# An adaLN block with hedgehog linear attention and a ReLU feed-forward on one core: the part before the feed-forward rewritten per 128-row tile, phi folded into weights, feed-forward matmuls reordered and interleaved

## The chip, the cores and the metric

The kernel runs on one core of a Trainium2 chip. The metric is the device time of that core in microseconds (us), lower is better. A time is quoted as a median of several runs; the profile belongs to one run, and its span is some 2 us shorter than the time of that run.

The engines are called as the profile calls them: PE is the matmul engine, PEld its weight load, DVE the vector engine, ACT the scalar (activation) engine, POOL the general engine, and SP, for which the pages show no busy time, issues transfers. "Granted clock" is the PE clock that the throttle allowed, 1.00 being full speed.

## The reference

S = 2048 rows, D = 576 features, 32 heads of 18, feed-forward width 4608, all bfloat16. Cut to what matters:

```python
sa, ca, ga, sb, cb, gb = split(silu(c) @ w_mod, 6)     # one row each
h = layernorm(x) * (1 + ca) + sa
q, k, v = heads(h @ wqkv)
pq, pk = q @ w_phi, k @ w_phi                          # 18x18 per head
phi_q = concat(softmax(pq), softmax(-pq))              # 36 features per head
phi_k = concat(softmax(pk), softmax(-pk))
kv, z = phi_k^T v, sum over rows of phi_k
o = (phi_q kv) / (phi_q z + 1e-6)
x = x + ga * (o @ wo)
h = layernorm(x) * (1 + cb) + sb
x = x + gb * (relu(h @ w1) @ w2)
```

576 is four and a half times 128. Both kernels therefore cut a contraction over features into four full matmuls over 128 features (`128*128` in the traces) and one "half" over 64 (`64*128`). They pair two halves, one in rows 0 to 63 and one in rows 64 to 127. For this pairing the kernels keep the last 64 features of each tensor a second time, in partitions 64 to 127.

## The kernel before

It runs in stages over the whole sequence. It loads all of x in one transfer, transposes it, computes the layernorm statistics with matmuls against ones, computes v, then loops over five groups of heads (seven heads, 126 columns, in a full one), computing q and k, phi, softmax and the attention of that group. Then come wo, a second layernorm over the whole sequence, and the feed-forward.

```python
nc.sync.dma_start(x_sb[:, :, :], xf.rearrange("(t p) d -> p t d", p=P))      # all of x
...
def dup_last_chunk():                      # the last 64 features again, by a transfer
    if PAIR:
        nc.gpsimd.dma_start(hT_sb[64:64 + kdl, cl, :], hT_sb[0:kdl, cl, :])
...
for g, (h0, nh) in enumerate(GRP):         # five head groups
    ...                                    # project q and k, cast them to qk_sb
    for tq in range(QT):                   # phi for q, then exp of both signs
        nc.tensor.matmul(pqp[0:nf, 0:SQ], lhsT=wbd[0:nf, 0:nf], rhs=qk_sb[0:nf, 0, sl], ...)
        nc.scalar.activation(out=Eq[0:nf, 0, sl], in_=pqp[0:nf, 0:SQ], func=ACT.Exp, scale=1.0)
        nc.scalar.activation(out=Eq[0:nf, 1, sl], in_=pqp[0:nf, 0:SQ], func=ACT.Exp, scale=-1.0)
    ...                                    # the same for k, its softmax, kv
    for tb in range(0, nT, NBN):           # both signs of q share ONE accumulator
        for sgn in range(2):
            nc.tensor.matmul(pnv[:, j, 0:nf + nh], lhsT=Eq[0:nf, sgn, t * P:(t + 1) * P],
                             rhs=KVZD[0:nf, sgn, 0:nf + nh], start=(sgn == 0), stop=(sgn == 1))
        ...                                # divide by one denominator per head
...                                        # transposes, dup_last_chunk, wo, second layernorm
dup_last_chunk()
for b in range(nTB):                       # feed-forward, 4 blocks of 512 rows
    while j < nKDF:                        # pairs of the 36 chunks of 128 hidden units
        for (jx, (js, jn)), hps in zip(js_list, hps_list):
            for ci, (st, kd) in enumerate(KD[:-1]):          # 8 full matmuls
                nc.tensor.matmul(hps[0:jn, :], lhsT=w1_sb[:kd, ci, js:js + jn],
                                 rhs=hT_sb[:kd, ci, b * TB:(b + 1) * TB], start=(ci == 0), stop=False)
        for idx, ((jx, (js, jn)), hps) in enumerate(...):    # 2 halves, rows 0 and 64
            b0 = 0 if idx == 0 else 64
            nc.tensor.matmul(hps[0:jn, :], lhsT=w1_sb[b0:b0 + kdl, cl, js:js + jn],
                             rhs=hT_sb[b0:b0 + kdl, cl, b * TB:(b + 1) * TB], start=False, stop=True)
        ...                                # relu, one chunk on ACT, one on DVE
    ...                                    # second matmul: 8 x 36 matmuls of 288 columns, then out
```

One detail of it is an approximation: the two softmaxes of q have normalisers of their own in the reference, while here the two signs are added without them and divided by one common denominator.

The softmax here doesn't subtract the row's maximum and nothing guards it: scores larger than these inputs give would overflow.

Of the kernel before, what the change touches and what calls it, by code (L numbers as in the profile page):

```python
# [7 lines left out]

STAGE = 99  # L10

P = 128
BF16 = mybir.dt.bfloat16
FP32 = mybir.dt.float32
EPS = 1e-5
# [3 lines left out]


def _chunks(n, c):
    out = []
    s = 0
    while s < n:
        out.append((s, min(c, n - s)))
        s += c
    return out
# [3 lines left out]
def kernel(  # L31
# [14 lines left out]
    B, S, D = A_x.shape  # L46
    assert B == 1
    H, Dh, _ = A_w_phi.shape
    Dff = B_w1.shape[1]
    assert D == H * Dh and Dh == 18, (D, H, Dh)  # L50
    nT = S // P
    assert S % P == 0
    KD = _chunks(D, P)
    nKD = len(KD)
    cl = nKD - 1
    stl, kdl = KD[cl]
    PAIR = (nKD >= 2 and kdl <= 64)
    KDF = _chunks(Dff, P)
    nKDF = len(KDF)
    NHG = P // Dh  # L60
    GRP = []
    hh = 0
    while hh < H:
        nh = min(NHG, H - hh)
        GRP.append((hh, nh))
        hh += nh
    NG = len(GRP)
    SQ = min(512, S)
    assert S % SQ == 0
    QT = S // SQ  # L70
    if S % 512 == 0:
        TB = 512
    elif S % 256 == 0:
        TB = 256
    else:
        TB = P
    nTB = S // TB
    NB = 4 if nT % 4 == 0 else (2 if nT % 2 == 0 else 1)
    CD = _chunks(D, 512)

    xf = A_x.flatten_outer_dims()
    outf = out.flatten_outer_dims()

    persist = ctx.enter_context(tc.tile_pool(name="persist", bufs=1))
    ident = persist.tile([P, P], BF16, name="ident")
    make_identity(nc, ident[:])
    onesb = persist.tile([P, P], BF16, name="onesb")
    nc.vector.memset(onesb[:], 1.0)
    eps_t = persist.tile([P, 1], FP32, name="eps_t")
    nc.vector.memset(eps_t[:], EPS)  # L90

    x_sb = persist.tile([P, nT, D], BF16, name="x_sb")
    nc.sync.dma_start(x_sb[:, :, :], xf.rearrange("(t p) d -> p t d", p=P))
    hT_sb = persist.tile([P, nKD, S], BF16, name="hT_sb")
    modcols = persist.tile([P, 6 * nKD], FP32, name="modcols")
    modrows = persist.tile([P, 2, D], FP32, name="modrows")
    mload = ctx.enter_context(tc.tile_pool(name="mload", bufs=1))
    ccol = mload.tile([P, nKD, 1], BF16, name="ccol")
    nc.vector.memset(ccol[:], 0.0)
    for ci, (st, kd) in enumerate(KD):  # L100
        nc.scalar.dma_start(ccol[:kd, ci, :], c[0:1, st:st + kd].rearrange("o k -> k o"))
    wmod_sb = mload.tile([P, nKD, 6 * D], BF16, name="wmod_sb")
    for ci, (st, kd) in enumerate(KD):
        nc.scalar.dma_start(wmod_sb[:kd, ci, :], w_mod[st:st + kd, :])

    actx = ExitStack()
    attn = actx.enter_context(tc.tile_pool(name="attn", bufs=1))
    wqkv_sb = attn.tile([P, nKD, 3 * D], BF16, name="wqkv_sb")
    for ci, (st, kd) in enumerate(KD):
        nc.sync.dma_start(wqkv_sb[:kd, ci, :], A_wqkv[st:st + kd, :])  # L110
    if PAIR:
        nc.sync.dma_start(wqkv_sb[64:64 + kdl, cl, :], A_wqkv[stl:stl + kdl, :])

    full_kd = [ci for ci, (st, kd) in enumerate(KD) if kd == P]
    assert nKD <= 8

    def transpose_tm_to_fm(src_tm_tile, t, pspool, dst):
        psraw = pspool.tile([P, 512], FP32, name="ps512")
        psT = psraw.bitcast(BF16)[:, 0:nKD * P].rearrange("p (c f) -> p c f", c=nKD)
        for ci, (st, kd) in enumerate(KD):  # L120
            nc.tensor.transpose(psT[:kd, ci, :], src_tm_tile[:, st:st + kd], ident[:, :])  # L121
        if full_kd:
            c0, c1 = full_kd[0], full_kd[-1] + 1
            nc.vector.tensor_copy(out=dst[:, c0:c1, t * P:(t + 1) * P], in_=psT[:, c0:c1, :])  # L124
        for ci, (st, kd) in enumerate(KD):
            if kd != P:
                nc.vector.tensor_copy(out=dst[:kd, ci, t * P:(t + 1) * P], in_=psT[:kd, ci, :])

    def dup_last_chunk():
        if PAIR:  # L130
            nc.gpsimd.dma_start(hT_sb[64:64 + kdl, cl, :], hT_sb[0:kdl, cl, :])

    def ln_pass1(rows_pool, pspool):
        xsq = rows_pool.tile([P, nKD, S], BF16, name="xsq", bufs=1)
        for ci, (st, kd) in enumerate(KD):
            nc.vector.tensor_tensor(out=xsq[:kd, ci, :], in0=hT_sb[:kd, ci, :], in1=hT_sb[:kd, ci, :], op=ALU.mult)
        ms, vs_ = [], []
        for tq in range(QT):
            sl = slice(tq * SQ, (tq + 1) * SQ)
            ps_s = pspool.tile([P, 512], FP32, name="ps512")  # L140
            ps_q = pspool.tile([P, 512], FP32, name="ps512")
            for ci, (st, kd) in enumerate(KD):
                nc.tensor.matmul(ps_s[:, 0:SQ], onesb[:kd, :], hT_sb[:kd, ci, sl],  # L143
                                 start=(ci == 0), stop=(ci == nKD - 1))
            for ci, (st, kd) in enumerate(KD):
                nc.tensor.matmul(ps_q[:, 0:SQ], onesb[:kd, :], xsq[:kd, ci, sl],  # L146
                                 start=(ci == 0), stop=(ci == nKD - 1))
            m = rows_pool.tile([P, 512], FP32, name="lnm")
            nc.scalar.activation(out=m[:, 0:SQ], in_=ps_s[:, 0:SQ], func=ACT.Copy, scale=1.0 / D)  # L149
            msq = rows_pool.tile([P, 512], FP32, name="lnmsq")  # L150
            nc.vector.tensor_tensor(out=msq[:, 0:SQ], in0=m[:, 0:SQ], in1=m[:, 0:SQ], op=ALU.mult)
            var = rows_pool.tile([P, 512], FP32, name="lnvar")
            nc.vector.scalar_tensor_tensor(out=var[:, 0:SQ], in0=ps_q[:, 0:SQ], scalar=1.0 / D,
                                           in1=msq[:, 0:SQ], op0=ALU.mult, op1=ALU.subtract)
            ms.append(m); vs_.append(var)
        lnvs = []
        for tq in range(QT):
            lnv = rows_pool.tile([P, 512], FP32, name="lnlnv")
            nc.scalar.activation(out=lnv[:, 0:SQ], in_=vs_[tq][:, 0:SQ], func=ACT.Ln, bias=eps_t[:], scale=1.0)
            lnvs.append(lnv)  # L160
        rss, nbs = [], []
        for tq in range(QT):
            rs = rows_pool.tile([P, 512], BF16, name="lnrs")
            nc.scalar.activation(out=rs[:, 0:SQ], in_=lnvs[tq][:, 0:SQ], func=ACT.Exp, scale=-0.5)  # L164
            rss.append(rs)
        for tq in range(QT):
            nb = rows_pool.tile([P, 512], BF16, name="lnnb")
            nc.vector.scalar_tensor_tensor(out=nb[:, 0:SQ], in0=ms[tq][:, 0:SQ], scalar=-1.0,
                                           in1=rss[tq][:, 0:SQ], op0=ALU.mult, op1=ALU.mult)
            nbs.append(nb)  # L170
        return rss, nbs

    def ln_apply(rows_pool, rss, nbs, scale_col, shift_col):
        for tq in range(QT):
            sl = slice(tq * SQ, (tq + 1) * SQ)
            rs, nb = rss[tq], nbs[tq]
            for ci, (st, kd) in enumerate(KD):
                t1 = rows_pool.tile([P, 512], BF16, name="lnt1")
                nc.vector.tensor_tensor(out=t1[:kd, 0:SQ], in0=hT_sb[:kd, ci, sl], in1=rs[:kd, 0:SQ], op=ALU.mult)  # L179
                nc.vector.tensor_tensor(out=t1[:kd, 0:SQ], in0=t1[:kd, 0:SQ], in1=nb[:kd, 0:SQ], op=ALU.add)  # L180
                if (tq * nKD + ci) % 2 == 0:
                    nc.scalar.activation(out=hT_sb[:kd, ci, sl], in_=t1[:kd, 0:SQ], func=ACT.Identity,  # L182
                                         scale=scale_col(ci, kd), bias=shift_col(ci, kd))
                else:
                    nc.vector.tensor_scalar(out=hT_sb[:kd, ci, sl], in0=t1[:kd, 0:SQ],  # L185
                                            scalar1=scale_col(ci, kd), scalar2=shift_col(ci, kd),
                                            op0=ALU.mult, op1=ALU.add)


    lctx1 = ExitStack()  # L190
    rows1 = lctx1.enter_context(tc.tile_pool(name="ln1rows", bufs=4))
    lnps1 = lctx1.enter_context(tc.tile_pool(name="ln1ps", bufs=4, space=bass.MemoryType.PSUM))
    for t in range(nT):
        transpose_tm_to_fm(x_sb[:, t, :], t, lnps1, hT_sb)
    rss1, nbs1 = ln_pass1(rows1, lnps1)

    with ExitStack() as mctx:
        modp = mctx.enter_context(tc.tile_pool(name="modp", bufs=1))
# [417 lines left out]
```

## Time and profile before

602.95 us, median of 4 runs (600.87 to 604.89).

These are lines of the page of the kernel before: its span, the busy time of PE with its share of the span, and three rows that cut the span into 40 equal slices (busy tenths of PE and DVE, and the granted clock in tenths).

```profile
span 602.0 us, 7761 instructions
...
PE 513.3 (85%) x3276; PEld 283.8 (47%) x3302; DVE 259.1 (43%) x589; ACT 148.5 (25%) x274; POOL 29.1 (5%) x36
...
PE   0899099799879598984089999999999999999997
...
DVE  0576934556956674797523211332123321133221
...
PEclk9995579797988759996679999999999999999999
```

85% busy looks almost full. The slices show two halves: PE is solid in the right half at clock 9, while the left half has gaps, and its clock sits between 5 and 9. The page therefore needs a table by stage. The next fence is the windows view of the kernel before: each row is a stretch of time, its length, the busy us of each engine with the number of instructions, the granted clock, and the share and rate of the transfers.

```profile
core 0: us, PE busy (x) PEld busy (x) DVE busy (x) ACT busy (x) POOL busy (x), PEclk, DMA share, GB/s
0.00:16.78 16.78, 0.00 (x0) 0.00 (x1) 0.35 (x4) 0.00 (x0) 3.79 (x28) 1.00 0.87 304
16.78:56.67 39.89, 38.33 (x288) 21.39 (x291) 25.84 (x64) 16.15 (x24) 0.00 (x0) 0.85 0.37 107
56.67:98.90 42.23, 27.49 (x157) 11.84 (x160) 28.50 (x64) 12.51 (x38) 0.66 (x1) 0.69 0.03 7
98.90:212.46 113.56, 92.80 (x631) 53.24 (x630) 69.51 (x156) 56.31 (x115) 23.60 (x5) 0.85 0.00 1
212.46:250.28 37.82, 34.98 (x232) 17.80 (x234) 22.61 (x68) 0.00 (x0) 0.57 (x1) 0.82 0.04 8
250.28:301.64 51.36, 25.00 (x137) 10.55 (x138) 38.10 (x99) 21.70 (x28) 0.51 (x1) 0.79 0.47 151
301.64:602.00 300.36, 294.72 (x1839) 169.02 (x1853) 74.16 (x136) 41.80 (x70) 0.00 (x0) 0.99 0.07 21
```

| stage (us) | what it does | PE idle, us | clock |
|---|---|---|---|
| 0 to 16.78 | load of x | 16.8 | - |
| 16.78 to 98.90 | transposes, statistics, modulation, v | 16.3 | 0.85, 0.69 |
| 98.90 to 212.46 | five head groups | 20.8 | 0.85 |
| 212.46 to 301.64 | wo, second layernorm | 29.2 | 0.82, 0.79 |
| 301.64 to 602.00 | feed-forward | 5.6 | 0.99 |

(PE idle is the length less the busy time.) Of 88.7 us of PE idle, 83 lie in the first half. The waits of PE in the kernel before, with what ended each, the total, how often, and the longest:

```profile
PE ps L121 <- DMA x_sb<-in_A_x_dram: 16.8, 1, 16.8
PE hps L560 <- DMA hT_sb<-hT_sb: 16.0, 1, 16.0
PE ps L315 <- ACT v_all L354: 14.4, 1, 14.4
PE hps L553 <- ACT hT_sb L182: 9.6, 1, 9.6
```

These four single waits make up 56.8 us: for x, for the copy of the last 64 features (it was issued at 294.6 us, when the whole second layernorm was done, and landed 7.0 us later), and twice behind a layernorm. The 9.6 us end with its last step. The 14.4 us end with an eviction of v that stands behind the first layernorm in the order of DVE and ACT; PE went on at 75.85 us. The weight load of its next halves waited for the first copy of the last 64 features until 75.99 us, so two waits end here almost together.

The feed-forward is bound by PE, and what can still be gained there is read in the timeline of PE (start us, us, line, shapes, how many; ends are modelled, so starts are to be compared). L553 are the full matmuls, L560 the halves:

```profile
312.38 0.39 PE L560 MATMUL hps<-hT_sb,w_sb 64*128 64x512 bf16 x2
312.70 1.90 PE L553 MATMUL hps<-hT_sb,w_sb 128*128 128x512 bf16 x8
314.53 0.39 PE L560 MATMUL hps<-hT_sb,w_sb 64*128 64x512 bf16 x2
```

A pair takes 314.53 - 312.38 = 2.15 us. Eight full matmuls and one slot of halves at 215 ns each are 1.94 us. The remaining 0.21 us are put down to two changes between full and half (changes of mode, or mode switches, below), some 0.107 us each: from the start of the halves to the next full matmul it is 0.32 us, about that much more than a slot.

### The profile page before, as it was taken

The numbers are of one execution on the slowest core, as the hardware profiler recorded it, in microseconds if no ns is written. First come the engines' busy times: TensorE is split into PE (matmuls) and PEld (weight loads), VectorE is DVE, ScalarE is ACT, GpSimd is POOL, SyncE is SP. The second block draws the span as 40 slices with busy tenths as digits, with TensorE's granted clock in tenths as the row PEclk, the third lists the DMA queues.
The fourth block names the chain that finished last, engine by engine and source line by source line (L and its number), as shares of the span: only waits on it lengthen the run. The fifth ranks groups of instructions, "written<-read, shape, count | busy, mean of one in ns | idle before, by whom it ended". The sixth has DMA issues, their size and how long they took to land.

```text
span 602.0 us, 7761 instructions
## 1 busy us (share of the span) xinstructions
PE 513.3 (85%) x3276; PEld 283.8 (47%) x3302; DVE 259.1 (43%) x589; ACT 148.5 (25%) x274; POOL 29.1 (5%) x36
## 2 busy tenths in 40 slices
PE   0899099799879598984089999999999999999997
PEld 0544044354444454531023577335773357733675
DVE  0576934556956674797523211332123321133221
ACT  0064322644644400046312100221002210022100
POOL 2000000013023200000000000000000000000000
PEclk9995579797988759996679999999999999999999
DMA  8910000000000000380380000000000000000000
GB/s 293 294 34 1 17 2 1 0 1 1 1 1 1 1 2 19 131 262 1 108 264 0 1 21 11 10 1 1 21 11 10 2 0 21 21 1 0 1 21 21
DMA packets 13651, 24.17 MB, mean 40 GB/s; under 512 B 2224, under 2 KB 11568, under 8 KB 12976
## 3 DMA queue, kind: packets, MB, share of 16 engines
q1 hardware_dynamic: 6704, 12.85, 6.5%
q10 hardware_dynamic: 6672, 10.03, 5.3%
q0 software_dynamic: 240, 0.79, 0.6%
q8 instruction: 26, 0.43, 0.3%
q14 instruction: 9, 0.07, 0.0%
HBM read 20.52 MB, written 2.36 MB: 38 GB/s over the span
## 4 chain that ended last, share of the span: by engine, by line
PE 56%; DVE 5%; ACT 1%; DMA 1%; issue 1%; DVEq 0%; POOLq 0%
PE hpsb L577 24%; PE hps L553 21%; PE hps L560 4%; PE ps L474 3%; PE ps L121 2%; DMA hT_sb<-hT_sb 1%; DVE lnt L180 1%; DVE lnt L179 1%; DVE hT_sb L124 1%; PE ps L146 1%; PE ps L143 1%; DVE hT_sb L185 1%; PE ps L481 1%; ACT L164 0%; PE psb L444 0%
## 5 line engine op out<-in xcount | busy, mean ns | idle before, releaser
L553 PE MATMUL hps<-hT_sb,w_sb 128*128 128x512 bf16 x560 | 139.5, 388 | 11.8 <-ACT hT_sb L182 9.6
L577 PE MATMUL hpsb<-w_sb,H 128*128 128x288 bf16 x1152 | 141.8, 286 | 0.0
L577 PEld LDWEIGHTS <-H 128*128 128x128 bf16 x1152 | 112.4, 98 | 29.1 <-issue 0.9
L566 ACT ACTIVATE H<-hps 128x512 bf16<-128x512 f32 x72 | 42.9, 597 | 227.5 <-PE hps L560 226.3
L568 DVE TENSOR_SCALAR H<-hps 128x512 bf16<-128x512 f32 x72 | 49.7, 691 | 113.7 <-PE hps L560 113.7
L553 PEld LDWEIGHTS <-w_sb 128*128 128x128 bf16 x576 | 51.5, 99 | 81.1 <-issue 31.9
L581 DVE TENSOR_TENSOR outt<-hpsb,modrows 128x288 bf16<-128x288 f32 x32 | 14.6, 457 | 116.3 <-PE hpsb L577 116.3
L370 PE MATMUL ps<-hT_sb,wqkv_sb 128*126 128x512 bf16 (+1 forms) x160 | 48.4, 442 | 2.1 <-ACT Ek L406 2.1
L560 PE MATMUL hps<-hT_sb,w_sb 64*128 64x512 bf16 x144 | 29.9, 394 | 16.0 <-DMA hT_sb<-hT_sb 16.0
L121 PE MATMUL ps<-ident,x_sb 128*128 128x128 bf16 (+1 forms) x160 | 20.8, 268 | 17.7 <-DMA x_sb<-in_A_x_dram 16.8
L315 PE MATMUL ps<-wqkv_sb,hT_sb 128*128 128x64 bf16 (+1 forms) x125 | 22.4, 324 | 15.8 <-ACT v_all L354 14.4
L370 PEld LDWEIGHTS <-wqkv_sb 128*126 128x126 bf16 (+1 forms) x160 | 21.6, 148 | 19.2 <-issue 12.3
L383 ACT CAST qk_sb<-ps 126x512 bf16<-126x512 f32 (+1 forms) x33 | 18.8, 592 | 46.4 <-PE ps L378 45.3
L124 DVE COPY hT_sb<-ps 128x512 bf16<-128x512 bf16 x48 | 20.3, 423 | 22.3 <-PE ps L121 22.2
L560 PEld LDWEIGHTS <-w_sb 64*128 64x128 bf16 x144 | 7.1, 93 | 48.0 <-issue 48.0
L415 POOL TENSOR_TENSOR Ek<-Ek,Rk 128x2016 bf16<-128x2016 bf16 (+1 forms) x5 | 23.6, 4721 | 110.9 <-DVE Rk L412 64.7
L121 PEld LDWEIGHTS <-x_sb 128*128 128x128 bf16 (+1 forms) x160 | 12.9, 115 | 25.5 <-DMA x_sb<-in_A_x_dram 16.8
L408 DVE TENSOR_REDUCE Dk<-Ek 128x28 f32<-128x504 bf16 (+1 forms) x40 | 22.3, 624 | 4.7 <-ACT Ek L405 4.7
L149 ACT ACTIVATE lnm<-ps 128x512 f32<-128x512 f32 x8 | 4.8, 597 | 76.6 <-PE ps L143 74.3
L474 PE MATMUL ps<-wo_sb,hT_sb 128*128 128x64 bf16 (+1 forms) x124 | 19.0, 290 | 1.9 <-DVE x_sb L490 1.6
L182 ACT ACTIVATE hT_sb<-lnt,modcols 128x512 bf16<-128x512 bf16 (+1 forms) x20 | 16.2, 813 | 14.9 <-DVE lnt L180 14.9
L490 DVE TENSOR_TENSOR x_sb<-x_sb,ps 128x512 bf16<-128x512 bf16 (+1 forms) x32 | 13.2, 450 | 12.3 <-PE ps L481 12.3
(87 smaller groups left out, 441.9 us busy)
## 6 DMA issues: line engine op xcount, KB each, us to landing
w_sb<-in_B_w_dram ACTq DMA_DIRECT2D x1, 5184.0 KB
w_sb<-in_B_w_dram SPq DMA_DIRECT2D x4, 1152.0 KB
wmod_sb<-in_w_mod_dram ACTq DMA_DIRECT2D x4, 864.0 KB
x_sb<-in_A_x_dram SPq DMA_DIRECT2D x1, 2304.0 KB
out_dram<-outt SPq DMA_DIRECT2D x16, 144.0 KB
wqkv_sb<-in_A_wqkv_dram SPq DMA_DIRECT2D x4, 432.0 KB
w_sb<-in_B_w_dram SPq DMA_DIRECT2D x2, 576.0 KB
hT_sb<-hT_sb POOLq DMA_DIRECT2D x3, 256.0 KB, 2.9
```

The lines of the kernel that those rows point to most:

```text
L121: nc.tensor.transpose(psT[:kd, ci, :], src_tm_tile[:, st:st + kd], ident[:, :])
L124: nc.vector.tensor_copy(out=dst[:, c0:c1, t * P:(t + 1) * P], in_=psT[:, c0:c1, :])
L315: nc.tensor.matmul(pvs[idx][:, 0:cn], lhsT=hT_sb[:kd, ci, t * P:(t + 1) * P], rhs=wqkv_sb[:kd, ci, colv0 + cs:colv0 + cs + cn], start=(ci ...
L370: nc.tensor.matmul(ps[0:nf, 0:SQ], lhsT=wqkv_sb[:kd, ci, col0:col0 + nf], rhs=hT_sb[:kd, ci, tq * SQ:(tq + 1) * SQ], start=(ci == 0), stop ...
L408: nc.vector.tensor_reduce(out=Dk[:, tb:tb + NB, sgn, 0:nh], in_=Ek[:, tb:tb + NB, sgn, 0:nf].rearrange("p b (h e) -> p b h e", e=Dh), axis ...
L415: eng.tensor_tensor(out=phik[:, :, sgn, 0:nf].rearrange("p t (h e) -> p t h e", e=Dh), in0=Ek[:, :, sgn, 0:nf].rearrange("p t (h e) -> p t ...
L474: nc.tensor.matmul(ps[:, 0:cn], lhsT=hT_sb[:kd, ci, t * P:(t + 1) * P], rhs=wo_sb[:kd, ci, cs:cs + cn], start=(ci == 0), stop=((not pairin ...
L553: nc.tensor.matmul(hps[0:jn, :], lhsT=w1_sb[:kd, ci, js:js + jn], rhs=hT_sb[:kd, ci, b * TB:(b + 1) * TB], start=(ci == 0), stop=((not pai ...
L560: nc.tensor.matmul(hps[0:jn, :], lhsT=w1_sb[b0:b0 + kdl, cl, js:js + jn], rhs=hT_sb[b0:b0 + kdl, cl, b * TB:(b + 1) * TB], start=False, st ...
L566: nc.scalar.activation(out=H1[0:jn, jx, :], in_=hps[0:jn, :], func=ACT.Relu)
L568: nc.vector.tensor_relu(H1[0:jn, jx, :], hps[0:jn, :])
L577: nc.tensor.matmul(ops_[:, 0:kn], lhsT=H1[0:jn, j, tt * P:(tt + 1) * P], rhs=w2_sb[0:jn, j, cols], start=(j == 0), stop=(j == nKDF - 1))
```

## The change

The intent is to remove the stages' hand-overs: work per tile of 128 rows instead of per sequence, so that engines overlap; do less of it (phi folded into the q and k weights, statistics on DVE instead of PE); write the last 64 features twice where they are produced, without a transfer; halve the changes of mode; and give PE feed-forward matmuls to do while the attention output waits for DVE. It also gives both signs of q their own normaliser, as the reference has it, which is additional work. The feed-forward arithmetic stays. The diff is nearly the whole file; its core:

```diff
-    nc.sync.dma_start(x_sb[:, :, :], xf.rearrange("(t p) d -> p t d", p=P))
+    nc.sync.dma_start(x_sb[:, 0, :], xf[:, 0, :])            # x in pieces, weights in between
+    nc.sync.dma_start(x_sb[:, 1, :], xf[:, 1, :])
+    load_rows(nc.sync, wk_raw, A_wqkv[:, D:2 * D], False)
+    ...
-    # transposes, ones-matmuls over hT_sb for the statistics
+    nc.vector.bn_stats(out=s[:, hf, :], in_=x_sb[:, t, hf * HD2:(hf + 1) * HD2])   # 2 per tile
-    # dup_last_chunk()
+    for a, b, src in ((0, 576, 0), (576, 640, 512)):         # layernorm writes 64 columns twice
+        nc.vector.tensor_scalar(out=y[:, a:b], in0=x_sb[:, t, src:src + b - a], ...)
-    # q, k -> cast -> phi matmul -> exp, per head group
+    fold_transposes(wk_raw, wkT, ...);  fold(wkT, wk_sb, ...)   # wk @ phi once; wq the same
+    for t in range(NT + 2):                                  # k/v loop, 16 tiles
+        k_tile(t); v_tile(t)                                 # matmul -> exp; matmul -> copy
+        k_softmax(t - 1)
+        kv_tile(t - 2)                                       # accumulates kv over the tiles
-    # one accumulator for both signs, one denominator
+    mm(p0, g * 140, g, 0) ...; mm(p1_, g * 140, g, 1) ...    # a bank for each sign
+    # 8 small ACT copies of the denominators and normalisers, then on DVE:
+    nc.vector.tensor_tensor(out=a[:, 0], in0=d[:, 0], in1=rev_pair(d[:, 1]), op=ALU.mult)
+    ...                                                      # A[sgn] = weight of each sign
+    nc.vector.tensor_tensor(out=o_sb[:, t % NO, :], in0=tm[:, 0, :], in1=tm[:, 1, :], op=ALU.add)
+    # per tile: num_tile, wo_tile, statistics, second layernorm
-            # 8 full, then 2 halves, for each pair
+            pair = (j, j + NJ // 2)
+            for part in ((full, halves) if j % 2 == 0 else (halves, full)):
+                part()
```

Laid out so, the PE stream has all 180 first-matmul instructions of feed-forward block 0 and 83 of the block's 288 second ones among those of the attention output.

## The prediction

> **What bounds it now.** The engine table gives PE (the matmul engine) 513 of 602 us, but in two regimes. From 302 us to the end (windows by stage) PE is 98% busy: four feed-forward blocks of 74.07 us, first matmul 38.6, second 35.4 (288 at 123 ns). The 302 us before are latency-bound: the chain of waits jumps between PE, ACT, DVE and DMA. PE waits 16.8 us for one load of all of x, 14.4 us in one wait behind the first layernorm, 9.6 us and a 16.0 us DMA wait before the feed-forward; the granted clock there is mostly 0.5 to 0.86.
>
> **What the change does.** A rewrite; only the feed-forward arithmetic stays.
>
> 1. Feed-forward. A pair of the first matmul takes 2.155 us: 8 full matmuls at 215 ns, two 64-row ones together (215 ns), leaving about 215 ns: two mode switches of some 107 ns. [...]320 ns from the 64-row pair's start to the next full matmul. The new order alternates full/half and half/full, so half of the switches go: 18 x 107 ns = 1.9 us, 72.2 us a block.
> 2. Attention. Phi is folded into the q and k weights, so separate projection and phi passes with their casts become one pass; k and v run per 128-row tile. Layernorm statistics move from ones-matmuls (80, 17 us of PE) to DVE. The duplicating DMAs go. Added: a correct normaliser for both signs of q, eight small ACT copies and more DVE work per tile.
> 3. The instruction order interleaves all of block 0's first feed-forward matmul and 83 of its 288 second ones into the attention output.
>
> **Sum.**
> - To the first k tile: about 2.6 MB must land (before moved 318 to 390 GB/s), then modulation columns (60 x 64 ns), transposes, evictions: 19 us.
> - k/v loop, 16 tiles. PE per tile: k 1.32, v 1.33, ten kv matmuls at 68 ns, five transposes at 101 ns: 3.8 us; plus 16.5 us of weight folds, q block and modulation: 78 us. ACT 64, DVE about 70 us (reduction of 1152 elements 1.35, reciprocal of 64 0.55, fitted to the trace's groups). PE-led, with hand-over stalls on few PSUM buffers: 88 us.
> - Attention output, 16 tiles. DVE about 6.7 us per tile (378-column multiplies 547 ns, 288-column adds 457 ns, fp32 add 0.75 us[...]): 107 us. PE 53 + 18 + 37 + 10 = 118 us. Both nearly full, fixed order: 124 us.
> - Rest: 205 x 0.123 + 3 x 72.2 + 3.7 us tail = 245.5 us.
>
> Total 476.5 us, about 21% faster, nearly all from the 302 us before the feed-forward: attention plus block 0's first half now end near 231 us. I expect 452 to 502 us.
>
> **What would show it.** Feed-forward blocks of 72.2 us, the second matmul still at 123 ns; DVE and PE each over 85% busy in the attention output; no 16 us DMA wait; PE over 85% busy in the k/v loop; total PE busy 430 to 450 us.
>
> **What would make it wrong.** Most of all the attention output: in PE's fixed order each stall of a DVE-dependent matmul also delays feed-forward matmuls behind it, and its stages share four PSUM buffers; 2 us more per tile is 32 us. Next, a throttled clock in a k/v loop with gaps (up to 20 us)[...]. In the other direction, my DVE durations may be too high.
>
> Chances: faster by over 2% 0.97, within 2% 0.02, slower 0.01.

In the sum this touches one term: DVE's layernorm statistics in the attention output. The 6.7 us per tile and the 107 us of DVE there still count it, and so the stage's 124 us and the total of 476.5 us stand as recorded, with a term cut from the list. The 107 ns of a mode switch are half of what is left of a pair's 2.155 us after nine slots of 215 ns.

## The result, and the profile after

The changed kernel takes 471.02 us (median of 10 runs, 469.82 to 472.78) against 603.0 us (15 runs of the kernel before, 600.43 to 605.73). The ratio is 0.7813, with a 95% interval of 0.7797 to 0.7829. Such a ratio is the mean time of one kernel's fast runs over that of the other's of the same rounds, so it is not quite the ratio of the quoted medians. It is 22% faster; 476.5 us was predicted, in a range of 452 to 502. All outputs are right.

The same lines of the page, of the kernel after:

```profile
span 469.3 us, 7860 instructions
...
PE 445.5 (95%) x3257; PEld 273.7 (58%) x3278; DVE 238.8 (51%) x569; ACT 160.9 (34%) x427; POOL 37.9 (8%) x51
...
PE   3898999999979999999999999999999999999996
...
DVE  5589973777959779698223332212332122332221
...
PEclk9999989999989999999999999999999999999999
```

The span fell by 132.7 us. By the two pages, PE's busy time fell by 67.8 us (513.3 to 445.5), and its idle time by 64.9 us (88.7 to 23.8). A part of the lower busy time is clock: over the span it rose from 0.906 to 0.993, and a matmul at a lower clock counts as busy for longer (in the kernel after, four of 288 columns take 0.66 us at 62.74 us, at a clock of 1.00, and 1.14 us at 66.91 us, at 0.50). DVE's row is now the denser one: 9 in several slices of the left half.

The windows view of the kernel after, in stages (columns as before): load and first preparations; k/v loop; attention output with the second layernorm and the interleaved feed-forward; the rest of the feed-forward.

```profile
0.00:21.19 21.19, 12.58 (x124) 10.99 (x124) 10.98 (x37) 5.80 (x13) 5.53 (x30) 1.00 0.95 301
21.19:105.00 83.81, 79.43 (x721) 52.84 (x720) 65.48 (x123) 52.43 (x110) 32.35 (x21) 0.98 0.33 111
105.00:223.46 118.46, 113.19 (x820) 62.41 (x829) 96.34 (x296) 68.98 (x248) 0.00 (x0) 0.99 0.11 38
223.46:469.30 245.84, 240.30 (x1597) 147.49 (x1607) 65.95 (x117) 33.69 (x56) 0.00 (x0) 1.00 0.03 10
```

PE is 95% busy in the k/v loop and 96% in the attention output, both at a clock of 0.98 or more. The waits of PE after; the first three of the list:

```profile
PE two L225 <- DMA rW<-in_A_wqkv_dram: 6.3, 1, 6.3
PE psa L272 <- DVE xn L263: 2.4, 3, 1.9
PE one L272 <- DVE rH L281: 1.4, 2, 1.0
```

The longest wait is now 6.3 us, for the k weights at the start, and no wait for a copy is left. The timeline of PE in the first feed-forward matmul (L529 full, L535 halves):

```profile
254.33 0.61 PE L535 MATMUL psf<-rEQ,rW 64*128 64x512 bf16 x4
254.87 3.63 PE L529 MATMUL psf<-rEQ,rW 128*128 128x512 bf16 x16
258.43 0.60 PE L535 MATMUL psf<-rEQ,rW 64*128 64x512 bf16 x4
```

Sixteen full matmuls and four halves follow on each other: two pairs take 258.43 - 254.33 = 4.10 us, against 4.31 for two pairs before, and there is one run of halves where there were two. A whole feed-forward block fell from 74.07 to 72.15 us, and the second matmul stayed at 122.5 ns each.

### The profile page after: what moved, and what is told of

It is laid out like the page before. It is cut to its first block, busy times and chain, and to the rows that moved or that the text cites. A ratio compares the mean times of both kernels' runs of the same rounds, so it can differ in the third digit from the quotient of the medians.

```text
span 469.3 us, 7860 instructions
## 1 busy us (share of the span) xinstructions
PE 445.5 (95%) x3257; PEld 273.7 (58%) x3278; DVE 238.8 (51%) x569; ACT 160.9 (34%) x427; POOL 37.9 (8%) x51
## 4 chain that ended last, share of the span: by engine, by line
PE 80%; DVE 11%; ACT 5%; DMA 1%; issue 1%; POOLq 0%; DVEq 0%
PE psf L551 30%; PE psf L529 24%; PE two L287 4%; PE psf L535 4%; PE psa L287 3%; PE psf L353 3%; DVE xn L263 2%; PE psa L452 2%; DVE R_sb L316 2%; DVE st L251 2%; PE one L196 1%; DMA x_sb<-in_A_x_dram 1%; PE kvacc L329 1%; DVE rH L320 1%; PE psa L291 1%
## 5 line engine op out<-in xcount | busy, mean ns | idle before, releaser
L551 PEld LDWEIGHTS <-rH 128*128 128x128 bf16 x1152 | 111.9, 98 | 29.2
L541 ACT ACTIVATE rH<-psf 128x512 bf16<-128x512 f32 x90 | 53.2, 602 | 182.1 <-PE psf L535 163.0
L551 PE MATMUL psf<-rW,rH 128*128 128x288 bf16 x864 | 112.9, 286 | 0.0
L529 PE MATMUL psf<-rEQ,rW 128*128 128x512 bf16 x420 | 96.7, 380 | 1.3 <-issue 0.9
L529 PEld LDWEIGHTS <-rW 128*128 128x128 bf16 x576 | 52.2, 98 | 66.3 <-issue 13.3
L543 DVE TENSOR_SCALAR rH<-psf 128x512 bf16<-128x512 f32 x54 | 37.3, 691 | 72.5 <-PE psf L535 36.8
L287 PE MATMUL two<-rW,rH 128*128 128x288 bf16 (+2 forms) x256 | 40.8, 298 | 1.2 <-ACT rH L278 0.4
L551 PE MATMUL psf<-rEQ,rH 128*128 128x288 bf16 x288 | 40.9, 286 | 0.0
L529 PE MATMUL psf<-rHT,rW 128*128 128x512 bf16 x135 | 37.1, 384 | 0.3 <-issue 0.2
L287 PEld LDWEIGHTS <-rH 128*128 128x128 bf16 x256 | 23.2, 101 | 9.1 <-ACT rH L278 0.9
L316 DVE TENSOR_REDUCE R_sb<-rH 128x64 f32<-128x1152 bf16 x16 | 21.5, 1344 | 13.4 <-ACT rH L302 13.3
L251 DVE BATCH_NORM_STATS2 st<-x_sb 128x6 f32<-128x288 bf16 x64 | 25.8, 438 | 3.5 <-DMA x_sb<-in_A_x_dram 3.5
L452 PE MATMUL psa<-kvzd,rEQ 126*128 126x140 bf16 (+1 forms) x160 | 15.9, 224 | 1.3 <-DVE rV L482 0.3
L452 PEld LDWEIGHTS <-rEQ 126*128 126x128 bf16 (+1 forms) x160 | 12.1, 100 | 8.5 <-issue 3.4
```

The source lines that it names most:

```text
L251: nc.vector.bn_stats(out=s[:, hf, :], in_=x_sb[:, t, hf * HD2:(hf + 1) * HD2])
L287: nc.tensor.matmul(ps(bk)[:, 0:cn], lhsT=lhs(ci, 0, P), rhs=rhs[:, ci, c0:c0 + cn], start=(ci == 0), stop=False)
L316: nc.vector.tensor_reduce(out=R[:, 0, :], in_=E, axis=AXX, op=ALU.add)
L452: nc.tensor.matmul(ps[:, col:col + w], lhsT=Eq[b][0:nf, g, sgn, tok], rhs=kvzd[0:nf, g, sgn, 0:w], start=True, stop=True)
L529: nc.tensor.matmul(hps[n][:], lhsT=w1a[:, ci, jj * P:(jj + 1) * P], rhs=h2T[b][:, ci, :], start=(j % 2 == 0 and ci == 0), stop=(j % 2 == 1 ...
L541: nc.scalar.activation(out=H1[:, jj, :], in_=hps[n][:], func=ACT.Relu)
```

## The experiments

Twelve kernels ran, in three sessions on different chips; the kernel before ran in each, at medians of 603.2, 603.6 and 603.9 us. A kernel derived from the one after is compared with its 471.02 us. Differences of about 1 us are not resolved by these runs, as the quoted intervals show. The theory to be tested is that the time is PE's total work plus the few gaps that are left, so that whatever fills a gap or removes PE work counts, and whatever shortens another engine's work counts little. The rival for the attention output was that DVE sets its pace, so that DVE work taken away there comes off the kernel's time one for one.

### 1 and 2. The order of full and half matmuls, alone

In the kernel after, the old order; in the kernel before, the new one:

```diff
 # after_noalt
-            for part in ((full, halves) if j % 2 == 0 else (halves, full)):
-                part()
+            full()
+            halves()
 # before_alt
+            first = (j // 2) % 2 == 0
+            for part in ((full, halves) if first else (halves, full)):
+                part()
```

> The changed kernel, with the first feed-forward matmul in one order for every pair (8 full matmuls, then the two 64-row ones), as before the change. Theory of mode switches: each of the 18 pairs of a block pays two switches of about 107 ns instead of one, so a block of 72.15 us goes back to 74.07 us and the whole kernel gains 4 x 1.9 = 7.7 us: 478.7 us. Rival: the shorter block comes from the new pairing of chunks (j with j+18) or from the evictions; then the block stays near 72.15 us and the kernel at 471 us.

> The kernel before, with only the alternating order (full, half, half, full) put into its first feed-forward matmul. Theory of mode switches: four blocks of 72.15 us instead of 74.07 us, 603.0 - 7.7 = 595.3 us. Rival (pairing or evictions shorten the block): no change, 603 us.

The kernel after with the old order took 478.29 us (ratio to before 0.7927, interval 0.7906 to 0.7949), 7.3 us more. The kernel before with the new order took 595.77 us (0.9878, 0.9846 to 0.9909), 7.4 us less than the 603.17 us of its session. Both agree with 4 x 18 x 0.107 = 7.7 us. The traces show it in the block itself: one takes 74.07 us in the first of these kernels and 72.15 in the second. The pairing of chunks is the new one in the first and the old one in the second, so the rival falls. The order of matmuls that are otherwise identical is worth this much in either kernel, and the cost of a change of mode is confirmed.

### 3. Without the interleave

The blocks of the feed-forward in the order 3, 0, 1, 2. Block 3 needs the last tiles of the attention output, so none of its matmuls can stand earlier.

```diff
-    for b in range(NB):
+    for b in (3, 0, 1, 2):
```

> The changed kernel, with the feed-forward blocks in the order 3, 0, 1, 2. Block 3 needs the last attention tiles, so no feed-forward matmul can stand among the attention output any more; the arithmetic is the same. Theory that filling PE's gaps is worth about 35 us: the attention output then runs at DVE's pace, 95 to 112 us instead of 118.5, the rest takes 4 x 72.15 + 3.7 = 292.3 us, total 492 to 509 us. Rival, that the interleaved feed-forward matmuls hold the attention up in PE's fixed order and nothing is gained by them: PE's own work of the attention output is some 57 us, so that stage falls to about 75 us and the total stays near 472 us.

It took 527.49 us (0.8738, 0.8715 to 0.8761): 56.5 us more, and more than the 492 to 509 us expected. The direction was right and the size was missed. The windows view of this kernel, two rows: the middle of the attention output, and all of it.

```profile
145.00:185.00 40.00, 27.94 (x168) 16.56 (x166) 29.90 (x92) 11.94 (x61) 0.00 (x0) 0.54 0.00 1
...
105.00:231.00 126.00, 88.73 (x566) 51.37 (x564) 95.82 (x293) 50.67 (x212) 0.00 (x0) 0.69 0.10 35
```

Two things make up 54 of the 56.5 us. The matmuls that no longer fit inside are 36.9 us of first and 83 x 0.1225 = 10.2 us of second matmul. The stage has become longer although it has fewer instructions: from 105 us to about 230.7, that is 125.7 us against 118.5. What changed in it is the clock: it was 0.69, and 0.54 in the middle, although the longest wait of PE in it is only 2.2 us. With 47 us of work moved out, PE was busy for 88.7 us where the other work of the stage, at full clock, is 113.2 less 47, some 66 us. The last 2 us lie after the stage and were not explained. This is the largest single part of the gain that was found.

### 4. One denominator instead of two

The attention output of the kernel after with the coarser normaliser of the kernel before: both signs accumulate in one bank, and 3 reciprocals and 3 multiplications replace 8 ACT copies and 9 DVE operations per tile.

```diff
-        for g in range(3):
-            mm(p0, g * 140, g, 0)
-        for g in range(3):
-            mm(p1_, g * 140, g, 1)
+        for g in range(3):
+            for sgn in range(2):
+                mm(p0, g * 140, g, sgn)          # start=(sgn == 0), stop=(sgn == 1)
 ...
-        d = dz[:, t % 2]                         # 8 ACT copies, ab products, two multiplies, one add
+        nc.vector.reciprocal(out=R[:, 0:21]..., in_=v0[:, :, 126:133])
+        nc.vector.tensor_tensor(out=o[:, 0:378]..., in0=v0..., in1=R..., op=ALU.mult)
```

> The changed kernel with the old kernel's coarser normaliser in the attention output: both signs accumulate in PSUM and one reciprocal serves both. The eight small ACT copies and about 2.5 of DVE's 6 us per tile go, PE's matmuls stay the same in number. Theory that PE (95% busy in this stage) sets the pace and DVE (81%) follows: at most the 5.3 us in which PE idles there can be won, 465 to 471 us, with the attention output shorter and fewer feed-forward matmuls inside it. Rival, that DVE's chain sets the pace: 16 x 2.5 = 40 us less, about 431 us.

It took 462.01 us (0.7658, 0.7626 to 0.769), 9.0 us less and 3 us below the expected 465 to 471. The windows view of it, the attention output:

```profile
105.00:191.60 86.60, 85.30 (x684) 48.58 (x684) 62.54 (x244) 48.55 (x107) 0.00 (x0) 1.00 0.15 50
```

The stage shrank from 118.5 to 86.6 us, and DVE's work in it from 96.3 to 62.5: both by about 32 to 34 us. The kernel gained 9. The reason is that the shorter stage hides less of the feed-forward: 12 of the 18 pairs (120 of 180 matmuls) of block 0's first matmul fit inside, and none of the second; the rest run later, at the same cost. What was gained is 4.8 us less PE idle over the whole span (23.8 to 19.0) and 4.2 us less PE busy. The rival, 431 us, is refuted. The idle time is what the expectation allowed for; the 4.2 us are what it missed, and why PE's busy time fell, with the same number of matmuls, was not found out. The variant also takes two of the four shared PSUM buffers for a tile's products where the kernel after takes three, so how much of the 32 us comes from the operations and how much from buffers that come free earlier is not separated.

### 5. Without the interleave, but with matmuls that nobody reads

To tell "the stage needs the time for its chain of hand-overs" from "PE's own work makes it long", experiment 3 with 192 matmuls of 512 columns as filler, whose result is never read: 192 x 0.215 = 41 us of useless work.

```diff
+    for b in range(1, NB):
+        for k in range(8):
+            junk = psf()
+            for i in range(8):
+                nc.tensor.matmul(junk[:], lhsT=w1a[:, i % 4, ...], rhs=h2T[b - 1][:, i % 4, :],
+                                 start=(i == 0), stop=(i == 7))
-    for b in range(NB):
+    for b in (3, 0, 1, 2):
```

> The kernel with feed-forward order 3, 0, 1, 2 (527.5 us, attention output 125.5 us long at a granted clock of 0.69), plus 192 matmuls of 512 columns on real data into PSUM tiles that nobody reads, which the scheduler puts into PE's gaps in the attention output; the result stays right. Theory that PE's idle gaps cost twice, by lowering the granted clock of the matmuls that DVE and ACT wait for: with 41 us of added PE work that stage gets shorter, to 105 to 118 us at a clock above 0.95, total 507 to 520 us. Rival, that DVE alone sets the pace of that stage at 125 us: it stays, and the total stays near 527 us or grows.

It took 520.28 us (0.8617, 0.8593 to 0.8642), 0.3 us above the expected 507 to 520: with 41 us of work more it was 7.2 us faster than without it. The windows view of it, from 105 us to the end of the attention output:

```profile
105.00:223.50 118.50, 107.97 (x750) 58.27 (x760) 95.17 (x292) 50.77 (x212) 0.00 (x0) 0.97 0.11 38
```

The stage ends at 223.5 us, just where it ends in the kernel after, with other filler and less PE work; and its clock is 0.97, not 0.69. So the stage's length, 7.4 us per tile, is not set by how much work fills PE. What is left is the chain of each tile through ACT, DVE and PE, and with experiment 4, which shortened that chain and the stage with it, this is the reading that fits. In experiment 3, where PE was left idle, the chain was longer: with the clock down to 0.54 from 145 to 185 us, the tile's own matmuls took longer (eight of 288 columns 2.10 us at 161.47 us, against 1.15 us at 130.56). In these experiments, then, the chain sets the stage's length, while the kernel's time follows PE's total work and what is left of its gaps. Which link of the chain binds was not tested.

### 6. The copy of the last 64 features in four pieces, in the kernel before

```diff
-    dup_last_chunk()
+    for q in range(QT):
+        nc.gpsimd.dma_start(hT_sb[64:64 + kdl, cl, q * SQ:(q + 1) * SQ],
+                            hT_sb[0:kdl, cl, q * SQ:(q + 1) * SQ])
```

> The kernel before, with the copy of the last 64 feature rows ahead of the feed-forward split into four, one for each 512 tokens, so that the first feed-forward block waits for its own quarter alone. Theory that the 16.0 us wait is one copy that starts after the whole second layernorm apply and then takes 7.0 us beside the weight load: the wait goes and the kernel gains 12 to 16 us, 587 to 591 us. Rival, that another wait of the same chain (layernorm apply on DVE, or the weights) ends at the same time: less than 4 us gained.

It took 594.64 us (0.9858, 0.9818 to 0.9898), 9.0 us less and not the 12 to 16 expected. The waits of PE in it that stand at the start of the feed-forward:

```profile
PE hps L554 <- ACT hT_sb L182: 9.6, 1, 9.6
PE hps L554 <- DVE H L569: 9.1, 2, 8.3
```

The transfer's 16.0 us are gone, but 8.3 us of them came back as a wait for DVE. The timeline of PE there:

```profile
283.08 0.39 PE L561 MATMUL hps<-hT_sb,w_sb 64*128 64x512 bf16 x2
291.79 1.44 PE L554 MATMUL hps<-hT_sb,w_sb 128*128 128x512 bf16 x3 [8.32 <-DVE H L569]
```

At 283.08 us the halves of an early pair are done; the next pair needs a relu on DVE, and the relu stands in DVE's order behind the layernorm of the later rows. Taking one wait away uncovered the next on the same path. In the kernel after, with its layernorm per tile, neither wait is left.

### 7. The kernel after with x in one transfer

```diff
-    nc.sync.dma_start(x_sb[:, 0, :], xf[:, 0, :])
+    nc.sync.dma_start(x_sb[:, :, :], xf[:, :, :])
 ...                                    # the four later pieces of x left out
```

> The changed kernel with x loaded whole, first in the queue, as the kernel before does, instead of in five pieces among the weights. 1.77 MB more then lie ahead of the key weights and modulation weights; at the 343 GB/s of this window that is 5.2 us. Theory that the lead-in waits for bytes: the first k tile starts 4 to 6 us later and the kernel takes 475 to 477 us. Rival, that the lead-in is a chain of small PE, ACT and DVE steps: under 2 us.

It took 479.38 us (0.7933, 0.7896 to 0.7969), 8.4 us more and above the expected 475 to 477. The wait of PE for the k weights:

```profile
PE two L221 <- DMA rW<-in_A_wqkv_dram: 13.1, 1, 13.1
```

The first matmul of the k/v loop starts at 26.92 us instead of 21.19, so 5.7 us come from the order of loads, as expected. The remaining 2.7 us were not expected. Between 60 and 105 us the clock was 0.89 instead of 0.96, which by an estimate is 45 x 0.07 = 3.2 us of PE time at full clock. The profiled run is the slowest of the four (480.91 us, mean clock 0.986); the fastest, at a mean clock of 0.993, took 477.31. So the clock fits the 2.7 us, but this was not tested.

### 8. The last 64 columns normalised once

The layernorm of the kernel after writes 64 columns twice with an extra DVE operation per tile. Instead, the transpose is done twice on PE:

```diff
-        for a, b, src in ((0, 576, 0), (576, 640, 512)):
+        # one tensor_scalar over 576 columns
 ...
+                        for r in range(2):
+                            nc.tensor.transpose(pt[64 * r:64 * r + 64, k, j * P:(j + 1) * P],
+                                                xn[:, (t0 + j) % NX, 512:576], ident[:, :])
```

> The changed kernel without the second normalise instruction per tile (64 columns, 346 ns, 32 times on DVE = 11.1 us): the last 64 features are transposed twice on PE instead (16 more transposes). Theory that DVE sets the pace only in the first part of the k/v loop, where it is 100% busy from 30 to 60 us, and PE elsewhere: some 2 to 4 us less, 467 to 469 us. Rival A, DVE sets the pace in the attention output too: 8 us or more. Rival B, PE everywhere: no gain, or a loss of 1 to 2 us from the added transposes.

This was a miss. DVE's busy time fell by 5.4 us (238.8 to 233.4), half of the 11.1 expected, and the kernel took 476.34 us (0.7887, 0.7861 to 0.7913), 5.3 us more. The timelines of PE just before 60 us, first of this kernel:

```profile
54.44 0.61 PE L272 MATMUL one<-ident,xn 128*128 128x128 bf16 x8
...
59.89 0.61 PE L272 MATMUL one<-ident,xn 128*128 128x128 bf16 x8 [2.75 <-DVE rH L285]
```

and of the kernel after:

```profile
55.64 0.61 PE L272 MATMUL one<-ident,xn 128*128 128x128 bf16 x8
...
58.97 0.61 PE L272 MATMUL one<-ident,xn 128*128 128x128 bf16 x8 [0.98 <-DVE rH L281]
```

The variant was 1.2 us ahead (its transposes start at 54.44 instead of 55.64), but then PE waited 2.75 us for a DVE eviction where the kernel after waits 0.98 us, and started the next transposes 0.9 us behind. After it, the clock between 60 and 105 us was 0.89 instead of 0.96. Close behind that wait six matmuls of 288 columns took 1.86 us (at 61.67 us) where the kernel after has 1.10 (at 60.88), and behind the 60 one-column matmuls of which experiment 11 tells, eight of 252 columns took 2.10 us (at 71.00 us), against 1.16 further on (at 76.02). The k/v loop ended near 108.5 us instead of 105, and 63 instead of 83 second matmuls stand in the attention output, (83 - 63) x 0.1225 = 2.5 us left for later. With the order fixed, 5.4 us less work on DVE moved where PE's gaps fell, and here they fell worse (2.75 us for 0.98). That the sequence of wait, lower clock and later end is one chain is argued and not shown.

### 9. Phi for q not folded into the weights

In the kernel after, the q weights are used as they are; each group of a q block gets a copy and a phi matmul more.

```diff
-            fold_transposes(wq_raw, wqT, "a")
-            fold(wqT, wq_sb, "a")
 ...
+                nc.scalar.activation(out=q, in_=pss[n][0:nf, :], func=ACT.Copy)      # or DVE
+                nc.tensor.matmul(pss[n][0:nf, :], lhsT=bdw[0:nf, g, 0:nf], rhs=q, start=True, stop=True)
```

> The changed kernel with phi no longer folded into the query weights: q is projected, cast to bf16 (half on ACT, half on DVE) and multiplied by the block-diagonal phi, as the kernel before did; the folding of the query weights goes. Estimate from this trace: PE loses 30 transposes and 25 small matmuls (about 5 us) and gains 20 matmuls of 512 columns (4.3 us); ACT loses about 8 us of evictions, ACT and DVE gain 20 casts of about 0.6 us. Theory that folding only swaps one cost for another at this size: within 4 us of 471 us. Rival, that folding is a main source of the gain: 480 us or more.

It took 481.87 us (0.7979, 0.7956 to 0.8002), 10.9 us more, so the fold is worth that, and the expectation of an equal time fell. PE's busy time differs only by 4.1 us. The windows view from 30 to 60 us, first of this kernel:

```profile
30.00:60.00 30.00, 23.48 (x197) 14.10 (x195) 29.84 (x47) 13.56 (x29) 14.87 (x11) 0.91 0.01 2
```

and of the kernel after:

```profile
30.00:60.00 30.00, 27.35 (x270) 18.89 (x267) 30.00 (x63) 21.89 (x48) 14.23 (x10) 1.00 0.01 3
```

In both, DVE is busy for practically the whole of these 30 us. The fold's transposes and matmuls lie here, in PE time that DVE would have left empty; without them PE is busy for 23.5 us instead of 27.4, and the clock is 0.91 instead of 1.00. The phi matmuls and copies that replace them come later. The k/v loop ended 7.3 us later (112.2 instead of 104.9), the attention output 10.9 us later (234.4 instead of 223.5). The sum of PE work in the estimate was about right; the place in time was not considered. That place and clock make the 10.9 us is read from the traces; no run separates them.

### 10 and 11. Two attempts to do better

Longer runs of halves, four pairs together in blocks 1 to 3 (after_wide), and the modulation's 60 one-column matmuls split into two groups of 30, four tiles (23 us) of the loop apart (after_split_mod):

```diff
 # after_wide, cut
+        for j in range(0, NJ // 2, 4):
+            full(j); full(j + 1)
+            halves(j); halves(j + 1); halves(j + 2); halves(j + 3)
+            ...                                  # then the full ones of j + 2 and j + 3
 # after_split_mod
-            mod_columns((3, 4), mod2)
+            mod_half(3, 0)
+        if t == 11:
+            mod_half(4, 1)
```

> The changed kernel with the 64-row matmuls of four pairs in one run instead of two, in feed-forward blocks 1 to 3 (the attention's PSUM banks are free by then): 5 runs of them a block instead of 9. Theory of mode switches: 4 x 2 x 107 ns = 0.86 us less a block, 2.6 us in all, 468.4 us, block time 71.3 us. Rival, evictions or PSUM hand-over bind once four pairs are open: no gain.

> The changed kernel with the 60 one-column matmuls for the second modulation columns, which stand in one run of 3.7 us, split into two runs of 30 four tiles apart. After that run the granted clock falls to 0.84 in the window 60 to 70 us and the next twelve k and v matmuls take about twice their time, 1.5 us in all. Theory that the run of tiny matmuls is what lowers the clock: 1 to 2 us less, about 469.5 us, and no dip there. Rival, the clock falls for another reason: dip and time stay.

The first took 470.61 us (0.78, 0.7775 to 0.7824), the second 470.15 us (0.7784, 0.776 to 0.7808); neither can be told from the kernel after. With longer runs, a group of four pairs takes 7.98 us instead of 8.19, two changes of mode less each, but the block's last run of halves now ends the block, and PE waits for the relu before the second matmul: 1.1 us in three waits, the longest 0.5 us. A block's first matmul takes 36.55 us instead of 36.87, so about 0.3 of the 0.86 us expected are left.

The split shows something else. The windows view of the kernel after, around its 60 one-column matmuls (63.24 to 66.98 us):

```profile
63.24:66.98 3.74, 3.74 (x63) 3.36 (x61) 2.68 (x6) 0.33 (x1) 1.47 (x1) 0.97 0.00 0
66.98:70.53 3.55, 3.55 (x17) 1.60 (x17) 2.18 (x7) 1.19 (x2) 0.00 (x0) 0.56 0.72 192
```

and of the kernel with the split, in the same stretches:

```profile
63.24:66.98 3.74, 3.74 (x47) 2.81 (x44) 3.63 (x10) 1.31 (x3) 1.58 (x1) 1.00 0.02 4
66.98:70.53 3.55, 3.55 (x34) 2.25 (x32) 2.98 (x5) 2.22 (x5) 1.02 (x1) 1.00 0.00 0
```

With 60 of them on end, PE is recorded as busy without a gap, and yet the clock falls to 0.56 for the 3.55 us that follow. With two groups of 30 it stays at 1.00, here and over the whole loop. So the dip went, as the theory had it; the 1 to 2 us less that it promised are not resolved.

An obvious rival is the transfer that runs in the second stretch of the kernel after (DMA share 0.72). The record speaks against it: with the split, the load comes later (DMA share 0.11 from 80 to 90 us, 0.96 from 90 to 100), beside a clock of 1.00. In the kernel before, 150 such matmuls run on end from 40.32 to 49.95 us; the clock is 0.99 to 45 us and 0.50 from there to 56.67, with a DMA share of 0.01. Experiments 3 and 5 keep the run of 60 in the loop of the kernel after, and their clock from 21 to 105 us is 0.98 as in that kernel; with the split, here and in experiment 12, it is 1.00 from 21.19 to 105 us.

### 12. A version that beats both

Experiments 4, 10 and 11 together (after_best).

> Wide runs, split modulation columns and the old kernel's one normaliser together. If the three are independent: 471.0 - 2.6 - 1.5 - 9.0 = 457.9 us. If the freed PE time of one is already in the other: 459 to 462 us.

460.05 us (0.7627, 0.76 to 0.7655), in the second of the two ranges. Two lines of its page:

```profile
span 457.0 us, 7660 instructions
...
PE 434.6 (95%) x3257; PEld 274.0 (60%) x3278; DVE 205.4 (45%) x521; ACT 146.2 (32%) x299; POOL 37.8 (8%) x51
```

The clock was 1.00 throughout in the profiled run. This is 11.0 us faster than the kernel after, and 9.0 of them are those of experiment 4; it has the normaliser of the kernel before, which is the coarser one. Who wants the reference's normaliser is left with about 470 us.

## Why the prediction was right

The predicted total and the sum's terms agree with what was measured (spans of the profile; the timed run is 1.7 us longer):

| term of the prediction | predicted, us | measured, us |
|---|---|---|
| to the first k tile | 19 | 21.2 |
| k/v loop | 88 | 83.8 |
| attention output | 124 | 118.5 |
| rest of the feed-forward | 245.5 | 245.8 |

- **The feed-forward.** 72.2 us a block were predicted and 72.15 measured. The cost of a change of mode, read from starts in one timeline, held in both directions (experiments 1 and 2): some 107 ns were added at each (1.92 us a block for 18 of them). What happens in PE at such a change was not shown.
- **The k/v loop.** PE was predicted to lead with 78 us of work; 79.4 were measured, with 4.4 us of gaps where 10 were allowed for. "PE-led" does not hold for the whole loop: from 30 to 60 us DVE is busy for 30.00 us and PE for 27.35. DVE came to 65.5 us (about 70 predicted), ACT to 52.4 us (64 predicted). The durations that were fitted from groups of the trace held: the reduction took 1344 ns (1.35 us predicted), the reciprocal of 64 columns 540 ns (0.55).
- **The attention output.** PE came to 113.2 us (118 predicted). DVE came to 96.3 us (107 predicted), which is 81% of the stage, and "over 85%" was wrong: 6.0 us per tile instead of 6.7. The large operations held (378 columns 547 ns as predicted, the fp32 addition 752 ns, the 288-column additions 445 instead of 457), so the excess lies in the operations that the sum did not list singly. The statistics, of which the trace before has no example, took 2 x 446 + 204 ns = 1.10 us (438 and 198 ns each as means over the whole kernel). For the addition of 576 fp32 columns, the straight line through two groups of the kernel before, 288 columns at 457 ns (L581) and 378 at 547 ns (L452), gives an estimate of 745 ns; 752 were measured.
- **What was feared.** That stalls of DVE-dependent matmuls would hold back feed-forward matmuls behind them did not come true to a large extent: PE lost 5.3 us in the stage. That a throttled k/v loop would cost up to 20 us did not come true in this kernel (clock 0.98), but in the variants of experiments 7 to 9 it was 0.89 to 0.91 from 60 to 105 us, and they took 5 to 11 us more; how much of that is the clock was not separated.
- **What the prediction did not see.** It counted the interleave as the 47 us of matmuls that it hides. It is worth 56.5 us: filling the gaps also kept the clock up (0.99 in the stage with it, 0.69 without, 0.97 with the filler of experiment 5), and the stage is 7 us shorter for it. And it spoke of PE and DVE as two full engines and took the longer. Experiments 4 and 5 show that they play different parts: the chain of each tile sets how long the stage is, PE's total sets how long the kernel is, and 32 us less of the first gave only 9 us of the second. That PE's work came near the stage's length is in part luck of the order: with 41 us of other filler in place of the 47 the stage was as long.

Where the 132 us came from, as far as single parts were tried: 7 us from the order of halves, 56 us from the interleave, and, each measured alone, 11 us from the fold of q and 8 us from the order of loads. About 9 us were also found by cutting the copy of the kernel before into pieces, which the change has no need of. The new normaliser costs 9 us. These do not add up exactly, as they share gaps. The rest, some 40 to 60 us by subtraction, is the work per tile in place of per sequence with its statistics on DVE and the fold of k; it was not divided further.

## What to carry to other kernels

When one stage leaves gaps on the engine that bounds the kernel, place independent matmuls of a later stage into them, and count the gain as the hidden work plus what the clock makes of it: here 47 us were hidden and 56.5 us gained, at a clock of 0.99 in the stage instead of 0.69. Before an operation is shortened or removed, ask which engine is full at that moment and whether the order can use the time: 32 us off one stage gave 9 us, 5.4 us less DVE work made the kernel 5.3 us slower, and 41 us of useless matmuls made one 7 us faster. Put full matmuls next to full ones and halves next to halves: in experiments 1 and 2 that was a matter of order alone, and each change of mode saved was worth some 107 ns in the traces.
